# Gated two-branch attention on one core: row halves in strict turn, stacks loaded a string earlier, differences one pair ahead, maxima transposed two bursts later

## The chip, the cores and the metric

The kernel runs on one core of one Trainium2 chip. The metric is the time of one execution in device microseconds (us). The kernel before has a median of 2800.9 us over three runs (2798.58 to 2801.37). Engines are named as in the profile: PE is the matrix engine (PEld its weight loads), DVE the vector engine, ACT the activation engine, POOL the general engine, SP the engine that issues most DMAs.

## The reference

Two attention blocks A and B with weights of their own read the same x, and a gate per token mixes them:

```python
def _A_ref(x, wqkv, wo):
    B, S, D = x.shape                    # 1, 2048, 512
    H = 32
    Dh = D // H                          # 16
    qkv = (lambda x, *d: x.transpose(*d))((x @ wqkv).reshape(B, S, 3, H, Dh), 2, 0, 3, 1, 4)
    q, k, v = qkv[0], qkv[1], qkv[2]
    scores = jnp.einsum("bhqd,bhkd->bhqk", q, k) * (Dh ** -0.5)
    p = _softmax(scores, axis=-1)
    o = jnp.einsum("bhqk,bhkd->bhqd", p, v)
    return (lambda x, *d: x.transpose(*d))(o, 0, 2, 1, 3).reshape(B, S, D) @ wo
...
x = A_x
g = _sigmoid((x * gate_w).sum(-1, keepdims=True))
a = _A_ref(x, A_wqkv, A_wo)
b = _B_ref(x, B_wqkv, B_wo)
return g * a + (1 - g) * b
```

So there are 64 heads (32 of A, 32 of B), each with 2048 x 2048 scores and a head width of 16. The softmax needs the maximum of each row of scores.

## The kernel before, in words

A prologue (to about 328 us) computes q, k and v of both blocks, splits q and k into two half-precision parts each, and writes them to DRAM. From there on the kernel is one long loop over 1024 rounds: 64 heads of 16 rounds. In round r of head h a block of 128 keys meets all 2048 queries.

**Stacks.** For a head, `load_stacks` (lines 103 to 122) puts the parts of q and k into the tiles `q_st` and `k_st`, 48 rows of parts, twice: on partitions 0 to 47 and again on 64 to 111. `x_st` holds differences of key halves. There are three q and k stacks and two of `x_st`, used in turn. The load is twelve DMAs on SP (L115 to L122, six for each half).

**Banks and row halves.** Scores are made one bank (128 x 512) at a time, by four matmuls on the 64-row half 0 or the half 64 of the PE array (`HALVES`), each on 32 columns. `rows()` (line 133) takes the halves in turn: `turn[0]` says which half is next. Matmuls on the two halves can run at the same time. There are four kinds of banks:
- "e", `score` (L218): the transposed scores of a key block; ACT takes the exponential of it (L220) into `p`. The row maxima enter as two more rows of the stack, so the exponent is already shifted.
- "m", `max_plain` (L153, then L159 on DVE): scores of a query block against 512 keys, and their maximum.
- "D", `max_rise` (L153 from `x_st`, then L166 on ACT): the positive part of the difference of two key quarters' scores, written to a buffer `rise`, of which there are three.
- "A", `max_pair` (L153, then L171 on DVE): scores of one quarter plus that `rise`, and the maximum of the sum, which is the maximum over both quarters. L171 writes into the same `rise` buffer.

**Bursts.** `attend` (L698) multiplies p by v in full precision. A head's sums stand in two PSUM tiles, `acc[0]` for half 0 and `acc[1]` for half 64, and a burst of n handles n blocks of 128 queries with both halves alternating, half 0 first. At a head's end ACT copies both tiles out (L721), POOL adds them (L723), and SP stores the sum to `od` (L724).

**The order.** Two rounds, a pair, are one string of steps: `Dmemme3eem2emmeeAe3`, where a digit is a burst. It has 16 banks: D, A, six m and eight e. Ahead of every burst `turn[0]` is set to 0, so the bank behind it takes half 0. An iteration of the loop is two strings, four rounds. The maxima run 24 rounds ahead of the scores that use them: a string whose scores are of round r makes the plain maxima and pairs of round r + 22 and the one behind it, and its "D" makes the difference of round r + 26, two pairs ahead of the "A" that uses it. The prologue makes the first two differences.

**At a head's border.** With r the first round of an iteration:
- r mod 16 = 2: the stacks of head r // 16 + 2 are loaded. On SP this comes behind the store of the head that has just ended. The first "D" of that head comes two strings later.
- r mod 16 = 6: the last maxima of a head are made; `max_split` and `max_rows` are put into `row_ops`, from which one is taken behind each burst.
- `max_split` (line 176): DVE takes the maximum over four columns (L180), POOL scales and splits it (L181 to L183).
- `max_rows` (line 186): DVE transposes the result (L188), SP writes it to DRAM (L191) and reads it back as two rows of `q_st` in both halves (L193). The head's first "e" needs these rows.

**Other work in the loop.** Work with a due round (`later`) is put in by `due`: loads of v for a group of eight heads (POOL's queue), reciprocals of the denominators (four, on DVE, through `row_ops`), and the output projections (L566), four tiles at a time ahead of a burst. The last 22 rounds have no maxima left and their own order.

Of the kernel before, what the change touches and what calls it, by code (L numbers as in the profile page):

```python
# [38 lines left out]
NT = S // P  # L39
# [4 lines left out]
NH = 2 * H  # L44
ROUNDS = NH * NT
# [4 lines left out]
HALVES = (0, 64)  # L50
# [4 lines left out]
def gated_mha(ctx: ExitStack, tc: tile.TileContext, xT, x, wqkv_a, wo_a, wqkv_b, wo_b, gate_w, out):  # L55
# [47 lines left out]
    def load_stacks(h, halves=HALVES):  # L103
        dma = nc.sync.dma_start
        s, hh = divmod(h, H)
        g, j = divmod(hh, HG)
        q, k = q_st[h % 3], k_st[h % 3]
        qs, ks, xs = qd[s][g], kd[s][g], xd[s][g]

        def pairs(t, step, n=S):  # L110
            v = t[0, j]
            return bass.AP(tensor=v.tensor, offset=v.offset, ap=[[n, DH], [step, 2], [1, n]])

        for b in halves:
            dma(k[b:b + 32], pairs(ks, HG * DH * S))  # L115
            dma(q[b:b + 32], pairs(qs, 0))
            dma(k[b + 32:b + 48], ks[0, j])
            dma(q[b + 32:b + 48], qs[1, j])
            if h:
                x = x_st[h % 2]  # L120
                dma(x[b:b + 32], pairs(xs, HG * DH * 512, 512))
                dma(x[b + 32:b + SC], xs[0, j])  # L122
# [6 lines left out]
    FIRST = NT + LEAD + 2  # L129
    mxp, rises = {}, {}  # L130
    turn = [0]

    def rows():
        turn[0] ^= 1
        return HALVES[1 - turn[0]]

    def new_maxima(h):
        mxp[h] = small.tile([P, NT, 4], F32, name="mxp")
        if h:
            pool.memset(mxp[h][:, FIRST % NT if h == 1 else 0::2, 1:2], LOWEST)  # L140

    def scores_bank(m, c, early=False):
        h, t = divmod(m, NT)
        st = c == "rise" or early and c % 2
        ps = (ps_st if st else ps_m).tile([P, 512], F32, name="ps_st" if st else "ps_m")
        b = rows()
        q = q_st[h % 3]
        if c == "rise":
            k = x_st[h % 2][b:b + SC]
        else:  # L150
            k = k_st[h % 3][b:b + SC, c * 512:(c + 1) * 512]
        for j in range(0, P, 32):
            pe.matmul(ps[j:j + 32], q[b:b + SC, t * P + j:t * P + j + 32], k, start=True, stop=True,  # L153
                      tile_position=(b, j))
        return ps, mxp[h][:, t]

    def max_plain(m, c, early=False):
        ps, o = scores_bank(m, c, early)
        dve.tensor_reduce(o[:, c:c + 1], ps, op=ALU.max, axis=AX.X)  # L159
# [3 lines left out]
    def max_rise(m):  # L163
        ps, _ = scores_bank(m, "rise")
        rises[m] = small.tile([P, 512], F32, name="rise", bufs=3)
        act.activation(rises[m], ps, AF.Relu)  # L166

    def max_pair(m):
        ps, o = scores_bank(m, 0)
        rise = rises.pop(m)  # L170
        dve.tensor_tensor_reduce(out=rise, in0=ps, in1=rise, scale=1.0, scalar=LOWEST,  # L171
                                 op0=ALU.add, op1=ALU.max, accum_out=o[:, 0:1])
# [26 lines left out]
    def result_bank():  # L199
        if ring:  # L200
            ring[0] = (ring[0] + 1) % 6
        if not ring or ring[0] % 2:
            return ps_m.tile([P, 512], F32, name="ps_m")
        return ps_st.tile([P, 512], F32, name="ps_st")

    def score(r, c):
        h, kt = divmod(r, NT)
        if c == 0:
            pt[r] = pro.tile([P, S], F32, name="raw") if r < 2 else ppool.tile([P, S], F32, name="p")
        q, k = q_st[h % 3], k_st[h % 3]  # L210
        kk, cc = (4 * (kt % 4) + c, kt // 4) if h == NH - 1 else (kt, c)
        b = rows()
        if r < 2 and c % 2:
            ps = ps_m.tile([P, 512], F32, name="ps_m")
        else:
            ps = result_bank() if ring else ps_st.tile([P, 512], F32, name="ps_st")
        for j in range(0, P, 32):
            pe.matmul(ps[j:j + 32], k[b:b + SC + 2, kk * P + j:kk * P + j + 32],  # L218
                      q[b:b + SC + 2, cc * 512:(cc + 1) * 512], start=True, stop=True, tile_position=(b, j))
        act.activation(pt[r][:, c * 512:(c + 1) * 512], ps, AF.Exp, scale=SCALE / UNIT ** 2)  # L220
# [13 lines left out]
    with tc.tile_pool(name="xs", bufs=1) as xs, tc.tile_pool(name="pro", bufs=2) as pro:  # L234
# [179 lines left out]
        for t in range(NT):  # L414
# [5 lines left out]
            elif t in (11, 13):  # L420
                turn[0] = 0
                for c in range(4):
                    score(t // 2 - 5, c)
        for i in range(2):
            turn[0] = 0
            max_rise(FIRST + 2 * i)
        assert not ahead


# [259 lines left out]
    def attend(r, qa, qb):  # L689
        h, kt = divmod(r, NT)  # L690
        v, j = vg[h // HG], h % HG
        p = pt[r]
        final = h == NH - 1
        a = kt % 4
        first, last = (a == 0, a == 3) if final else (kt == 0, kt == NT - 1)
        for c in range(NQ):
            for i, b in enumerate(HALVES):
                pe.matmul(acc[i][32 * c:32 * c + 17, qa * P:qb * P], v[b:b + 64, 4 * a + c if final else kt, j],  # L698
                          p[b:b + 64, c * 512 + qa * P:c * 512 + qb * P], start=first and qa == 0, stop=last,
                          tile_position=(b, 32 * c), skip_group_check=True)  # L700
        if qb < 4:
            return
        del pt[r]
        if final and last:
            hi = work.tile([P, 512], F32R, name="ev_hi", tag="num")
            lo = work.tile([P, 512], F32R, name="ev_lo")
            ev = work.tile([P, 512], F32, name="ev")
            act.copy(ev, acc[0])
            dve.tensor_tensor(ev, acc[1], ev, op=ALU.add)
            if kt == NT - 1:  # L710
                act.copy(hi, ev)
                dve.tensor_tensor(lo, ev, hi.bitcast(F32), op=ALU.subtract)
            else:
                pool.tensor_copy(hi, ev)
                pool.tensor_tensor(lo, ev, hi.bitcast(F32), op=ALU.subtract)
            tail[kt // 4] = (hi, lo)
        elif last:
            G, j = divmod(h, HG)
            parts = [work.tile([P, 512], F32, name=n) for n in ("ev_lo", "ev")]
            for i in range(2):  # L720
                act.copy(parts[i], acc[i])  # L721
            ev = parts[1]
            pool.tensor_tensor(ev, parts[0], ev, op=ALU.add)  # L723
            nc.sync.dma_start(od[G][j].rearrange("c r t -> (c r) t"), ev)  # L724
# [15 lines left out]
    projects, row_ops = [], []  # L740

    def due(first):
        for r in (first, first + 1):
            for fn, a in later.pop(r, ()):
                if fn is project_out:
                    projects.append(a)
                else:
                    fn(*a)

    first = 2 + NT + LEAD  # L750
    plain = ((m + c // 4, c % 4) for m in range(first, ROUNDS, 2) for c in range(2, 8))
    pairs = iter(range(first, ROUNDS, 2))
    to_rise = iter(range(first + 4, ROUNDS, 2))

    load_stacks(2)
    r = 2
    while r < ROUNDS:
        m = r + NT + LEAD
        if m >= ROUNDS and not ring:
            ring.append(5)  # L760
            turn[0] = 0
        order = (EDGE if r % NT == 2 and r > 2 else FULL)[0] + (EDGE if r % NT == 14 else FULL)[1]
        if m >= ROUNDS:
            order = LATE
        n = order.count("e") // 4
        due(r)
        if r % NT == 2 and r // NT + 2 < NH:
            if r // NT:
                load_stacks(r // NT + 2)
            new_maxima(r // NT + 2)  # L770
        scored = bursts = 0
        for step in order:
            if step == "e":
                if scored == 8:
                    due(r + 2)
                score(r + scored // 4, scored % 4)
                scored += 1
            elif step == "m":
                max_plain(*next(plain))
            elif step == "D":  # L780
                for k in to_rise:
                    max_rise(k)
                    break
            elif step == "A":
                max_pair(next(pairs))
            else:
                for a in projects:
                    project_out(*a)
                projects.clear()
                turn[0] = 0  # L790
                attend_next(int(step))
                if row_ops:
                    fn, *a = row_ops.pop(0)
                    fn(*a)
                for fn, a in mid.pop((r, bursts), ()):
                    fn(*a)
                bursts += 1
        if m < ROUNDS and (m + 4) % NT == 0:
            row_ops += [(max_split, m // NT), (max_rows, m // NT)]
        r += n  # L800
    attend_next(4)
    for fn, a in mid.pop((ROUNDS - 2, 2)):
# [29 lines left out]
```

## Time and profile before

| | us |
|---|---|
| median of three runs | 2800.9 |
| the profiled execution | 2808.05 |
| its span | 2806.3 |
| PE busy | 2657.5 (95%) |
| ACT busy | 2417.1 (86%) |
| DVE busy | 2369.4 (84%) |
| POOL busy | 354.7 (13%) |

Busy time counts an instruction from its start to its end. Consecutive ones overlap on ACT and DVE, and matmuls of different parts of the array run at the same time, so an engine can be busy all the time and still wait. Idle time is put down to the engine whose signal came last. In the timeline equal instructions that follow each other stand in one row with their count.

### The profile page before, as it was taken

To read this page: it belongs to the slowest core of one execution; us is meant where nothing else is said; L and a number is where in the kernel's file an instruction comes from. 1 tells how busy PE (TensorE), PEld (TensorE's weight loads), DVE (VectorE), ACT (ScalarE), POOL (GpSimd) and SP (SyncE) were. 2 spreads that over 40 slices of the span, in tenths; PEclk is the share of its full clock that TensorE was granted. 3 is DMA by queue.
4 is the path that set the end of the run, shared out by engine and by line. 5 is a ranking of instruction groups with operands and counts; after the bars stand their busy time and mean duration, and the time that the engine had idled before them with its cause. 6 is when DMAs were issued, how large, how long until landed. Compare 5 with 4: busy or idle time off the path is not lost.

```text
span 2806.3 us, 147881 instructions
## 1 busy us (share of the span) xinstructions
PE 2657.5 (95%) x66710; PEld 1511.1 (54%) x66710; DVE 2369.4 (84%) x4474; ACT 2417.1 (86%) x4862; POOL 354.7 (13%) x594
## 2 busy tenths in 40 slices
PE   9999999999999999999999999999999999999998
PEld 7777555555455555555455555555555545545553
DVE  4434799999899999999899878899899989998784
ACT  4122799999999999999999878899999999998696
POOL 1010112220000000000100323000000011002212
PEclk9999999999999999999999999999999999999999
DMA  5352212111111111111211212111211121122102
GB/s 197 110 158 96 66 45 65 52 46 38 49 41 31 30 40 49 37 39 37 60 36 32 97 57 75 33 34 29 53 37 38 38 56 42 31 58 75 49 24 93
DMA packets 95934, 159.62 MB, mean 57 GB/s; under 512 B 26182, under 2 KB 43974, under 8 KB 95302
## 3 DMA queue, kind: packets, MB, share of 16 engines
q1 hardware_dynamic: 91590, 139.68, 16.1%
q8 instruction: 522, 8.55, 1.3%
q0 software_dynamic: 2560, 8.91, 1.3%
q10 hardware_dynamic: 1152, 1.57, 0.2%
q14 instruction: 110, 0.90, 0.1%
HBM read 100.56 MB, written 49.54 MB: 53 GB/s over the span
## 4 chain that ended last, share of the span: by engine, by line
PE 42%; ACT 37%; DVE 9%; issue 8%; DMA 2%; POOL 1%; SPq 1%; POOLq 0%; ACTq 0%
ACT p L220 33%; PE acc L698 15%; PE ps_st L218 8%; DVE mxp L159 6%; PE ps_st L298 6%; PE ps_m L153 3%; PE ps_st L351 3%; PE ps_m L566 3%; PE ps_st L153 3%; ACT rise L166 2%; ACT ev_lo L721 2%; DVE rise L171 1%; DMA x_st<-xd 1%; POOL mrow L181 1%; DMA q_st<-qd 1%
## 5 line engine op out<-in xcount | busy, mean ns | idle before, releaser
L220 ACT ACTIVATE p<-ps_st 128x512 f32<-128x512 f32 x4044 | 2055.9, 651 | 98.3 <-PE ps_st L218 86.8
L159 DVE TENSOR_REDUCE mxp<-ps_m 128x1 f32<-128x512 f32 x3048 | 1899.5, 682 | 210.6 <-PE ps_st L153 94.5
L218 PE MATMUL ps_st<-q_st,k_st 50*32 50x512 f16 x16192 | 1517.7, 383 | 86.1 <-ACT p L220 3.9
L698 PE MATMUL acc<-p,vg 64*17 64x384 f32 (+1 forms) x32320 | 1390.4, 382 | 13.3 <-issue 4.4
L153 PE MATMUL ps_m<-k_st,q_st 48*32 48x512 f16 x14192 | 1244.7, 384 | 13.1 <-DVE mxp L171 12.3
L218 PEld LDWEIGHTS <-k_st 50*32 50x32 f16 x16384 | 627.5, 90 | 824.7 <-issue 735.3
L698 PEld LDWEIGHTS acc<-p,vg 64*17 64x17 f32 x32320 | 557.6, 93 | 126.3 <-ACT ev_lo L721 25.0
L153 PEld LDWEIGHTS <-q_st 48*32 48x32 f16 x16384 | 436.3, 90 | 239.6 <-issue 162.7
L166 ACT ACTIVATE rise<-ps_st 128x512 f32<-128x512 f32 x500 | 306.4, 613 | 50.8 <-DVE mxp L171 30.7
L171 DVE CUSTOM_DVE_ANT_0 rise<-ps_m,rise 128x512 f32<-128x512 f32 x500 | 340.3, 681 | 1.3 <-PE ps_m L153 1.3
L153 PE MATMUL ps_st<-x_st,q_st 48*32 48x512 f16 x2000 | 201.4, 378 | 14.8 <-DMA q_st<-qd 7.7
L723 POOL TENSOR_TENSOR ev<-ev_lo,ev 128x512 f32<-128x512 f32 x63 | 80.2, 1274 | 1057.0 <-ACT ev L721 1057.0
L181 POOL TENSOR_SCALAR mrow<-mrow 128x16 f32<-128x16 f32 x64 | 16.4, 256 | 992.7 <-DVE mrow L180 992.7
L318 ACT ACTIVATE parts<-ps_st 128x512 f16<-128x512 f32 x64 | 38.0, 596 | 112.1 <-PE ps_st L298 105.4
L319 DVE SCALAR_TENSOR_TENSOR parts<-ps_st,parts 128x512 f16<-128x512 f32 x64 | 44.0, 690 | 96.1 <-ACT parts L318 89.9
L354 ACT COPY v_st<-ps_st 128x512 f32<-128x512 f32 x32 | 18.8, 586 | 99.0 <-PE ps_st L351 96.6
L566 PE MATMUL ps_m<-wo,ot 128*128 128x512 f32 x348 | 85.5, 401 | 2.7 <-DVE mxp L159 2.7
L566 PEld LDWEIGHTS ps_m<-wo,ot 128*128 128x128 f32 x348 | 65.8, 192 | 23.4 <-issue 8.7
L298 PE MATMUL ps_st<-xh,whi 128*128 128x512 f32 x224 | 59.9, 390 | 0.0
L298 PE MATMUL ps_st<-xh,wlo 128*128 128x512 f32 x224 | 59.9, 390 | 0.0
L298 PE MATMUL ps_st<-xl,whi 128*128 128x512 f32 x224 | 59.9, 390 | 0.0
L553 POOL TENSOR_TENSOR o_num<-o_num,rb 128x512 f32<-128x512 f32 x28 | 35.7, 1280 | 95.6 <-DMA rb<-rd 95.6
(120 smaller groups left out, 1005.2 us busy)
## 6 DMA issues: line engine op xcount, KB each, us to landing
k_st<-kd SPq DMA_DIRECT2D x128, 128.0 KB
q_st<-qd SPq DMA_DIRECT2D x128, 128.0 KB
od<-ev SPq DMA_DIRECT2D x63, 256.0 KB
vd<-v_st SPq DMA_DIRECT2D x32, 272.0 KB
vg<-vd POOLq DMA_DIRECT2D x32, 272.0 KB, 4.6
qd<-parts SPq DMA_DIRECT2D x32, 256.0 KB
kd<-parts SPq DMA_DIRECT2D x32, 256.0 KB
k_st<-kd SPq DMA_DIRECT2D x128, 64.0 KB
```

Source lines behind the costliest of these rows:

```text
L153: pe.matmul(ps[j:j + 32], q[b:b + SC, t * P + j:t * P + j + 32], k, start=True, stop=True, tile_position=(b, j))
L159: dve.tensor_reduce(o[:, c:c + 1], ps, op=ALU.max, axis=AX.X)
L166: act.activation(rises[m], ps, AF.Relu)
L171: dve.tensor_tensor_reduce(out=rise, in0=ps, in1=rise, scale=1.0, scalar=LOWEST, op0=ALU.add, op1=ALU.max, accum_out=o[:, 0:1])
L218: pe.matmul(ps[j:j + 32], k[b:b + SC + 2, kk * P + j:kk * P + j + 32], q[b:b + SC + 2, cc * 512:(cc + 1) * 512], start=True, stop=True, ti ...
L220: act.activation(pt[r][:, c * 512:(c + 1) * 512], ps, AF.Exp, scale=SCALE / UNIT ** 2)
L298: pe.matmul(ps, w[a][:, k], (xh, xl)[b][cc][:, k], start=n == 0, stop=n == 3 * KC - 1)
L351: pe.matmul(ps, a[:, k, o:o + P], b[:, k], start=n == 0, stop=n == 3 * KC - 1)
L566: pe.matmul(ps, ot[a][:, slot, tt * P:(tt + 1) * P], wt[b][:, g], start=first and i == 0, stop=last and i == 2)
L698: pe.matmul(acc[i][32 * c:32 * c + 17, qa * P:qb * P], v[b:b + 64, 4 * a + c if final else kt, j], p[b:b + 64, c * 512 + qa * P:c * 512 + ...
L721: act.copy(parts[i], acc[i])
L723: pool.tensor_tensor(ev, parts[0], ev, op=ALU.add)
```

## The change

Four edits. The line numbers behind them fall by one or two.

```diff
-        for i in range(2):
-            turn[0] = 0
-            max_rise(FIRST + 2 * i)
+        max_rise(FIRST)
...
         for c in range(NQ):
-            for i, b in enumerate(HALVES):
+            for i in (turn[0], 1 - turn[0]):
+                b = HALVES[i]
                 pe.matmul(acc[i][32 * c:32 * c + 17, qa * P:qb * P], v[b:b + 64, 4 * a + c if final else kt, j],
...
-    to_rise = iter(range(first + 4, ROUNDS, 2))
+    to_rise = iter(range(first + 2, ROUNDS, 2))
...
         if r % NT == 2 and r // NT + 2 < NH:
-            if r // NT:
-                load_stacks(r // NT + 2)
             new_maxima(r // NT + 2)
...
                 if scored == 8:
                     due(r + 2)
+                    if (r + 2) % NT == 0 and r // NT + 3 < NH:
+                        load_stacks(r // NT + 3)
...
-                turn[0] = 0
                 attend_next(int(step))
                 if row_ops:
                     fn, *a = row_ops.pop(0)
-                    fn(*a)
+                    if fn:
+                        fn(*a)
...
-            row_ops += [(max_split, m // NT), (max_rows, m // NT)]
+            row_ops += [(max_split, m // NT), (None,), (None,), (max_rows, m // NT)]
```

**Halves.** `turn[0]` is no longer set to 0 ahead of a burst, and a burst begins with the half whose turn it is. In the string, six banks stand ahead of the first burst, three ahead of the second and seven ahead of the third. Before, the bank just ahead of the second and of the third burst was on half 0, and the burst began with half 0 too; the bank behind the burst took half 0 again. Now two neighbours never share a half. Since the prologue makes one difference and not two, each "D" falls on half 64. On PE, at the third burst of a string, before (acc_74 belongs to half 0, acc_75 to half 64):

```order
L218 LDWEIGHTS k_st_163
L218 MATMUL ps_st<-q_st_162,k_st_163 32x512
L698 MATMUL acc_74<-p,vg 17x384
L698 MATMUL acc_75<-p,vg 17x384
L698 MATMUL acc_74<-p,vg 17x384
```

And now:

```order
L218 LDWEIGHTS k_st_163
L218 MATMUL ps_st<-q_st_162,k_st_163 32x512
L697 MATMUL acc_75<-p,vg 17x384
L697 MATMUL acc_74<-p,vg 17x384
L697 MATMUL acc_75<-p,vg 17x384
```

The score ahead of the burst is on half 0 in both; the burst began with half 0 and now begins with half 64, and so does the "D" behind it.

**Differences.** "D" makes the difference of the next pair and not of the one behind that. With three buffers, the one it writes was last read by an "A" two strings back; before, by the "A" of the string just ended.

**Maxima.** Between `max_split` and `max_rows` two bursts are passed without a row operation. On DVE at the border of a head, before (L159 is a plain maximum, the two rows of L171 are one pair):

```order
L180 TENSOR_REDUCE mrow<-mxp 128x16
L159 TENSOR_REDUCE mxp<-ps_m 128x1
L188 STREAM_TRANSPOSE mt<-mparts 128x32
L159 TENSOR_REDUCE mxp<-ps_m 128x1 x2
L171 ISA rise,mxp<-ps_m,rise 128x512
L171 ISA mxp 128x1
L159 TENSOR_REDUCE mxp<-ps_m 128x1 x6
```

And now:

```order
L180 TENSOR_REDUCE mrow<-mxp 128x16
L159 TENSOR_REDUCE mxp<-ps_m 128x1 x3
L171 ISA rise,mxp<-ps_m,rise 128x512
L171 ISA mxp 128x1
L159 TENSOR_REDUCE mxp<-ps_m 128x1 x3
L188 STREAM_TRANSPOSE mt<-mparts 128x32
L159 TENSOR_REDUCE mxp<-ps_m 128x1 x3
```

The transpose moved behind five more maxima and the pair between them.

**Stacks.** The load of head h + 3's stacks is issued in the middle of the iteration r mod 16 = 14, just behind the last scores of head h, whose stack it overwrites. On SP around a head's border, before:

```order
L191 DMA md_114<-mt 4x32x32
L193 DMA q_st_2668<-md_114 2x2048 x2
L724 DMA od_108<-ev 128x512
L115 DMA k_st_168<-kd_90 32x1x2048
L116 DMA q_st_167<-qd_82 32x1x2048
```

And now:

```order
L191 DMA md_114<-mt 4x32x32
L193 DMA q_st_2661<-md_114 2x2048 x2
L115 DMA k_st_168<-kd_90 32x1x2048
L116 DMA q_st_167<-qd_82 32x1x2048
L117 DMA k_st_168<-kd_90 16x2048
```

The store of the ended head's sums (L724, now L723) stood ahead of the twelve loads and now stands behind them.

## The prediction

> **What bounds the kernel now.** I read the page first, then ACT's time by stage, then what ACT waited for in each stage, then single pairs of rounds in the timeline, and last the queue of SP. By the page's shares PE, DVE and ACT are all nearly full, which does not tell which one sets the pace. The timeline of ACT over one pair in the middle of a head tells it (start, length, line, count):
>
> ```profile
> 1513.72 1.17 ACT L220 ACTIVATE p<-ps_st 128x512 f32<-128x512 f32 x2
> 1514.81 0.60 ACT L166 ACTIVATE rise<-ps_st 128x512 f32<-128x512 f32 x1
> 1515.30 4.02 ACT L220 ACTIVATE p<-ps_st 128x512 f32<-128x512 f32 x8
> 1519.22 0.60 ACT L166 ACTIVATE rise<-ps_st 128x512 f32<-128x512 f32 x1
> ```
> ```profile
> 1515.30 0.59 ACT L220 ACTIVATE p<-ps_st 128x512 f32<-128x512 f32 x1
> ```
>
> Eight exponentials end 4.02 - 0.59 = 3.43 us apart from first to last, so ACT finishes one in 0.490 us when it is fed. A pair has nine operations: 9 x 0.490 = 4.41, and the two rises end at 1515.41 and 1519.82, 4.41 apart. So in the middle of a head ACT is already full. A head is 64 exponentials, 8 rises and 2 copies of the accumulators: 74 x 0.490 = 36.26 us. What a head takes is seen from one transpose (L188) to the next:
>
> ```profile
> 1113.76 0.21 DVE L188 STREAM_TRANSPOSE mt<-mparts 128x32 f16<-128x32 f16 x1 [0.35 <-POOL mparts L183]
> ```
> ```profile
> 1148.74 3.54 ACT L220 ACTIVATE p<-ps_st 128x512 f32<-128x512 f32 x7
> 1149.60 0.21 DVE L180 TENSOR_REDUCE mrow<-mxp 128x16 f32<-128x64 f32 x1
> 1149.72 0.68 DVE L159 TENSOR_REDUCE mxp<-ps_m 128x1 f32<-128x512 f32 x1
> 1150.76 0.21 DVE L188 STREAM_TRANSPOSE mt<-mparts 128x32 f16<-128x32 f16 x1 [0.35 <-POOL mparts L183]
> 1150.89 1.25 DVE L159 TENSOR_REDUCE mxp<-ps_m 128x1 f32<-128x512 f32 x2
> 1150.99 0.57 SPq L191 DMA_DIRECT2D md<-mt  x1
> 1152.05 0.68 DVE L171 CUSTOM_DVE_ANT_0 rise<-ps_m,rise 128x512 f32<-128x512 f32 x1
> 1152.84 0.60 ACT L166 ACTIVATE rise<-ps_st 128x512 f32<-128x512 f32 x1 [0.55 <-DVE mxp L171]
> 1152.97 0.52 SPq L193 DMA_DIRECT2D q_st<-md  x2
> ```
>
> It is 37.00, so 0.74 over ACT's floor, and the rows show nearly all of it in one place: the last exponential ends at 1152.28, the rise ends at 1153.44 and not 0.49 later, a loss of 0.67. The rise waited for L171 (end 1152.73), which frees the rise buffer it is to write; L171 was late because DVE had stood still for POOL (0.35) before L188.
>
> How much ACT loses in all is its count at 0.490 against each stage's length (us, then busy and count), with what it waited for in the first and third stage:
>
> ```profile
> 327.70:1604.00 1276.30, 1241.45 (x2516) 0.99 0.16 46
> 1604.00:1799.00 195.00, 147.17 (x299) 1.00 0.19 58
> 1799.00:2512.00 713.00, 693.80 (x1407) 1.00 0.15 42
> 2512.00:2694.30 182.30, 147.04 (x298) 0.98 0.19 57
> ```
> ```profile
> ACT rise L166 <- DVE mxp L171: 18.2, 35, 0.6
> ACT rise L166 <- PE ps_m L153: 8.3, 4, 3.4
> ACT p L220 <- PE ps_st L218: 4.2, 6, 1.0
> ACT rise L166 <- PE ps_st L153: 2.5, 1, 2.5
> ```
> ```profile
> ACT rise L166 <- PE ps_m L153: 6.3, 3, 2.5
> ACT p L220 <- PE ps_st L218: 1.9, 2, 1.0
> ```
> ```profile
> ACT p L220 <- PE ps_st L218: 45.1, 4, 11.3
> ```
> ```profile
> ACT p L220 <- PE ps_st L218: 29.3, 5, 8.8
> ACT p L220 <- PE ps_m L153: 5.5, 3, 2.8
> ```
>
> The first stage loses 1276.3 - 1232.8 = 43.5, the third 713.0 - 689.4 = 23.6. The second loses 48.5, of which 45.1 stand behind the four output projections (last but one fence), leaving 3.4; the fourth loses 36.3, of which 34.8 (last fence) are of that sort, leaving 1.5. Together 72.0 us are in reach of the change. Of them 8.3 + 4.2 + 2.5 + 6.3 + 1.9 = 23.2 belong to rises that waited for a matmul, and to exponentials just behind them; these are the heads whose stacks came late.
>
> **The strict turn.** PE's last burst of a string (L698) and the start of the next string, and DVE beside it:
>
> ```profile
> 1513.49 1.02 PE L698 MATMUL acc<-p,vg 64*17 64x384 f32 x16
> 1514.15 0.43 PE L153 MATMUL ps_m<-k_st,q_st 48*32 48x512 f16 x4
> 1514.33 0.40 PE L153 MATMUL ps_st<-x_st,q_st 48*32 48x512 f16 x4
> ```
> ```profile
> 1514.77 0.40 PE L153 MATMUL ps_m<-k_st,q_st 48*32 48x512 f16 x4
> 1514.94 0.40 PE L218 MATMUL ps_st<-q_st,k_st 50*32 50x512 f16 x4
> ```
> ```profile
> 1514.63 0.08 DVE L171 DVE_READ_ACCUMULATOR2_ANT mxp<- 128x1 f32 x1
> 1514.84 3.68 DVE L159 TENSOR_REDUCE mxp<-ps_m 128x1 f32<-128x512 f32 x6
> ```
>
> The last "e" and the first matmuls of the burst behind it (1513.49) now share a half, and "D" needs the same half: its matmuls start at 1514.33, after those of the "m" behind it in the program, which took the other half at 1514.15. They end at 1514.73, and the rise could not start before about 1514.78, which is also where ACT's turn falls (1514.89 + 0.49 - 0.60). So "D" is on the edge. With strict turn "D" takes the half that is free first, starts at about 1514.15 and is 0.18 early; "m" then starts at 1514.33, and since DVE's first reduction waited for "D" until 1514.84, it starts when it did. PE executes as many matmuls as before. The second and third burst change places of halves in the same way, where PE has to wait for ACT's banks anyway. Behind a head's end the first burst now begins with the accumulator that is copied second; the exponentials of the two copies' time cover that. By itself this edit is worth 0.00 to 0.03 a pair, at most 500 x 0.03 = 15 us; I count it in the sum only as what keeps the next edit from stopping at "D".
>
> **Differences one pair ahead.** Three rise buffers stay. The rise now overwrites the one that L171 read two strings ago, not one, so that wait has a whole pair (4.41) of room. No work is added; one rise moves from the prologue into the loop: +0.5.
>
> **Maxima transposed two bursts on.** DVE's insertion was 1150.89 - 1149.60 less one reduction of 0.60, so 0.69, in one place. Now L180 costs 0.12 (1149.60 to 1149.72) and L188 0.13 (1150.76 to 1150.89), a pair apart, and POOL's work lies beside reductions. DVE has 0.13 idle a pair (1514.71 to 1514.84 above). Its delay reaches ACT only by the third "m" (1514.77, waits for L171's bank) and the "e" behind it (1514.94): 0.17 of room. I take 0.05 a head, 62 x 0.05 = 3; bounds 0 and 62 x 0.25 = 16. In the seven heads with reciprocals these now follow L188 burst upon burst: 2, bounds 0 and 7 x 0.6 = 4 (one reduction's time a head).
>
> What is late next is the scores of the next head, which need the maxima's rows:
>
> ```profile
> 1161.42 0.40 PE L218 MATMUL ps_st<-q_st,k_st 50*32 50x512 f16 x4
> ```
>
> L188 to this matmul: 10.66. L188 moves by three reductions, L171 and three more, 0.12 + 1.80 + 0.81 + 1.80 - 1.16 = 3.4, and ACT's 0.67 goes: 6.6 stay. Needed: L188 to the second L193 is 2.5 (1150.76 to about 1153.23), and a write of the same 8 KB took 1.98 from issue until L193 could start (1150.99 to 1152.97): 4.5. Room 2.1. Behind these DMAs on SP wait only the next stack's, which are due later.
>
> **Stacks at a head's first round.** The load's first DMA stands behind the store of od on SP; its time, and the old head's last score on PE:
>
> ```profile
> 1507.87 0.56 SPq L115 DMA_DIRECT2D k_st<-kd  x1
> ```
> ```profile
> 1499.24 0.40 PE L218 MATMUL ps_st<-q_st,k_st 50*32 50x512 f16 x4
> ```
>
> Now it waits only for the old head's last score, the matmuls of 1499.24: 8.2 earlier. The first use, "D" of the new head, comes one string later: 4.4. Together 12.6 us of room where the longest wait was 3.4. Twelve issues, 6.7 us at L115's 0.56, now stand ahead of od's store; they are through about when it was ready (8.2 later), and its reader is behind it on SP anyway.
>
> **The sum.** 72.0 less 0.5, 3, 2 and 3 for strays that I cannot place: 63.5. The profiled execution took 2808.05 (span 2806.3), so 2744.5 there. The median is 2800.9, 7.15 below; if that whole difference is load waits that profiling lengthened, the gain is 56, if none of it, 63.5. I take 2738.
>
> The Trainium skill speaks against all this: by "ScalarE: Activation LUTs", What ACT_TABLE_LOAD costs, an ACTIVATE with immediate scale and bias takes 186 ns + 0.833 ns an element and overlaps its neighbour by 93, so 520 ns here, and a head could not be under 38.5; by it ACT has nothing to lose and the time stays. The trace disagrees (0.490, and heads of 37.00).
>
> **The rivals.**
> - *The delay comes back through PE.* DVE's two inserts, though apart, push the third "m" and so the exponentials, and half of 62 x 0.67 returns: +21, 2759. For it: the room is only 0.17, and PE is in order. 0.15.
> - *Loads stay late.* The group's value loads share the DMA engines with the stacks, and they now begin together: +23, 2761. Against: 12.6 of room. 0.07.
> - *More goes.* Of the fourth stage 34.8 - 3 x 8.8 = 8.4 are not projections: 2730. 0.08.
> - *Slower: the maxima land late.* At the first "e" of each head PE waits for L193. It pays from 6.6 us after L188, and eats the whole gain from 7.6 (62 x 1.0). Once the trace shows that much:
>
> ```profile
> 1701.98 0.55 SPq L191 DMA_DIRECT2D md<-mt  x1
> 1708.15 0.53 SPq L193 DMA_DIRECT2D q_st<-md  x2
> ```
>
>   There the path is 0.24 + 6.17 + 0.26 + 1.98 = 8.65. In every head this would be 62 x 2.05 = 127: 2865. Against: output loads filled the queue there. 0.05.
> - *No change.* ACT's 74 operations fill a head by themselves, at 37.00 / 74 = 0.50 each, and the 0.67 only moves to another wait of ACT: 2800. Against: pairs of 4.41. 0.05. The page above is of this side.
>
> **The numbers.** The forecast has 0.60, at 2738 with bounds 2729 (all 72 kept) and 2753 (the inserts at 16, the reciprocals at 4). With the rivals up to 2761 the range is 2726 to 2764. About 0.2% (5.6 us) can be told from no change: faster 0.90, same 0.05, slower 0.05.
>
> **What would show it.** L188 without idle time before it; rises that wait for L171 gone; the "D" matmuls ahead of the next "m"; heads of 36.3 to 36.5 from one L188 to the next; no rise that waits over 1 us for a matmul. It is wrong if the exponentials wait for L218 once in each head, or if ACT's operations in a pair end more than 4.41 apart.

## The result, and the profile after

The changed kernel takes 2724.1 us (median of four runs, 2723.3 to 2724.6); the kernel before took 2801.1 on the same chip (2798.6 to 2804.3). The ratio is 0.9724, with a 95% interval of 0.9707 to 0.9741, so it is faster by 77 us. The forecast was 2738 and its range began at 2726: the direction and the main mechanism hold, but the gain is larger than the range allowed. The profiled execution of the changed kernel took 2724.6 (span 2722.8), that of before 2808.0: 83.5 between the two profiles, where the sum gave 63.5.

The page's groups of the two lines that stood at the rise buffer. The last figures are the idle time ahead of them:

```profile
L166 ACT ACTIVATE rise<-ps_st 128x512 f32<-128x512 f32 x500 | 357.2, 715 | 0.0
L171 DVE CUSTOM_DVE_ANT_0 rise<-ps_m,rise 128x512 f32<-128x512 f32 x500 | 340.6, 681 | 0.0
```

Over 500 rises ACT never waited for one. The timeline at a head's border shows why, DVE first, then ACT, then PE's line L153:

```profile
1123.70 0.21 DVE L180 TENSOR_REDUCE mrow<-mxp 128x16 f32<-128x64 f32 x1
1123.83 1.88 DVE L159 TENSOR_REDUCE mxp<-ps_m 128x1 f32<-128x512 f32 x3
1125.62 0.68 DVE L171 CUSTOM_DVE_ANT_0 rise<-ps_m,rise 128x512 f32<-128x512 f32 x1
1126.23 0.08 DVE L171 DVE_READ_ACCUMULATOR2_ANT mxp<- 128x1 f32 x1
1126.31 1.89 DVE L159 TENSOR_REDUCE mxp<-ps_m 128x1 f32<-128x512 f32 x3
1128.11 0.20 DVE L188 STREAM_TRANSPOSE mt<-mparts 128x32 f16<-128x32 f16 x1
```
```profile
1126.19 0.72 ACT L166 ACTIVATE rise<-ps_st 128x512 f32<-128x512 f32 x1
1126.68 4.14 ACT L220 ACTIVATE p<-ps_st 128x512 f32<-128x512 f32 x8
1130.60 0.72 ACT L166 ACTIVATE rise<-ps_st 128x512 f32<-128x512 f32 x1
```
```profile
1125.67 0.42 PE L153 MATMUL ps_st<-x_st,q_st 48*32 48x512 f16 x4
1125.86 0.40 PE L153 MATMUL ps_m<-k_st,q_st 48*32 48x512 f16 x4
```

L188 no longer stands still for POOL (no bracket behind it). The rise of 1126.19 starts while L171 of this pair is still at work, since it fills another buffer. "D" (the first PE row) runs ahead of the next "m". The next rise comes 4.41 later: a pair at a head's border is now as short as one in the middle. The next head's transpose:

```profile
1164.38 0.20 DVE L188 STREAM_TRANSPOSE mt<-mparts 128x32 f16<-128x32 f16 x1
```

1164.38 - 1128.11 = 36.27: the floor of 74 x 0.490 = 36.26. ACT's time by stage (start and end, length, busy and count, PE's granted clock, share and GB/s of DMA), and then all that ACT waited for from 329.4 to 2623 (total, times, longest):

```profile
329.40:1527.50 1198.10, 1197.56 (x2444) 1.00 0.16 46
1527.50:1718.00 190.50, 145.12 (x296) 1.00 0.22 67
1718.00:2444.70 726.70, 726.08 (x1481) 1.00 0.15 43
2444.70:2621.20 176.50, 145.21 (x296) 1.00 0.19 57
```
```profile
ACT p L220 <- PE ps_st L218: 77.3, 8, 11.5
```

At 0.490 each, the operations of the first stage need 1197.6 of 1198.1, those of the third 725.7 of 726.7. Over the whole loop ACT waits eight times, for the eight groups of output projections (four of four tiles, three of three and one of two: 27 tiles, 2.86 each). Beside these it loses about 0.24 in each of the seven heads with reciprocals. PE itself waits 0.57 once a head, 35.5 in all, for the second copy of the accumulators (`ev`, L720), since the first burst now begins there. The prediction said that ACT's exponentials would cover this, and they do: ACT has no wait for it.

### The profile page after: what moved, and what is told of

It is laid out like the page before. It is cut to its first block, busy times and chain, and to the rows that moved or that the text cites. A ratio compares the mean times of both kernels' runs of the same rounds, so it can differ in the third digit from the quotient of the medians.

```text
span 2722.8 us, 147771 instructions
## 1 busy us (share of the span) xinstructions
PE 2577.0 (95%) x66710; PEld 1521.8 (56%) x66710; DVE 2361.3 (87%) x4474; ACT 2401.3 (88%) x4862; POOL 355.4 (13%) x594
## 4 chain that ended last, share of the span: by engine, by line
PE 73%; ACT 17%; DVE 7%; issue 2%; DMA 1%; SPq 0%; DVEq 0%; ACTq 0%
PE acc L697 30%; PE ps_st L218 20%; ACT p L220 15%; PE ps_m L153 9%; PE ps_st L298 6%; DVE mxp L159 6%; PE ps_st L351 3%; PE ps_m L564 3%; ACT ev L720 2%; PE ps_st L153 1%; DVE rise L171 1%; DMA x_st<-xd 0%; DVE rn L520 0%; DMA raw<-in_xT 0%; PE ps_st L564 0%
## 5 line engine op out<-in xcount | busy, mean ns | idle before, releaser
L220 ACT ACTIVATE p<-ps_st 128x512 f32<-128x512 f32 x4044 | 2105.1, 725 | 82.3 <-PE ps_st L218 77.8
L159 DVE TENSOR_REDUCE mxp<-ps_m 128x1 f32<-128x512 f32 x3048 | 1893.0, 682 | 160.5 <-PE ps_m L153 64.8
L697 PE MATMUL acc<-p,vg 64*17 64x384 f32 (+1 forms) x32320 | 1367.6, 379 | 39.3 <-ACT ev L720 35.5
L153 PE MATMUL ps_m<-k_st,q_st 48*32 48x512 f16 x14192 | 1118.7, 380 | 1.7 <-DVE mxp L171 1.3
L218 PEld LDWEIGHTS <-k_st 50*32 50x32 f16 x16384 | 636.8, 89 | 834.4 <-issue 712.9
L153 PEld LDWEIGHTS <-q_st 48*32 48x32 f16 x16384 | 444.1, 89 | 145.8 <-issue 57.0
L166 ACT ACTIVATE rise<-ps_st 128x512 f32<-128x512 f32 x500 | 357.2, 715 | 0.0
L171 DVE CUSTOM_DVE_ANT_0 rise<-ps_m,rise 128x512 f32<-128x512 f32 x500 | 340.6, 681 | 0.0
L153 PE MATMUL ps_st<-x_st,q_st 48*32 48x512 f16 x2000 | 210.4, 377 | 0.0
L298 PEld LDWEIGHTS ps_st<-xh,wlo 128*128 128x128 f32 x224 | 42.0, 188 | 8.8
```

What stands on the lines that cost most here:

```text
L298: pe.matmul(ps, w[a][:, k], (xh, xl)[b][cc][:, k], start=n == 0, stop=n == 3 * KC - 1)
```

## The experiments

Times are medians of four runs; the kernel before, run beside them in four groups, had 2801, 2803, 2802 and 2802. Each diff is against the kernel named.

### One edit undone

**no_turn**: the changed kernel with the fixed halves.

```diff
-            for i in (turn[0], 1 - turn[0]):
-                b = HALVES[i]
+            for i, b in enumerate(HALVES):
...
+                turn[0] = 0
                 attend_next(int(step))
```

> The changed kernel with the halves as before (turn set to 0 ahead of each burst, a burst begins with half 0). Theory of the prediction: the D matmuls fall back to about 0.18 us later, on the edge of ACT's turn, but no longer behind a wait for L171, so 0.00 to 0.03 us a pair: 2724 to 2739 us, likeliest 2726, heads of 36.26 to 36.5 us. Rival, that the steady pairs owe their time to the strict turn: heads lose 0.3 us or more, 2745 us or more.

Measured 2726.9, ratio 0.9735 (0.9720 to 0.9749). The intervals of the two ratios overlap, so the 2.8 more are not clear of the noise: beside the other three edits the turn is worth almost nothing.

**no_later_maxima**: the transpose one burst behind the maxima.

```diff
-            row_ops += [(max_split, m // NT), (None,), (None,), (max_rows, m // NT)]
+            row_ops += [(max_split, m // NT), (max_rows, m // NT)]
```

> The changed kernel with the transpose one burst behind the maxima, as before. Theory of the prediction: DVE again loses 0.69 us at one place; with the rise free of L171 some 0.35 us of it is covered, so 0.34 us a head comes back: 62 x 0.34 = 21, about 2745 us. Rival A, the free rise buffer alone hides all of it: 2724 us. Rival B, the whole 0.67 us returns: 2765 us.

Measured 2751.2, ratio 0.9819 (0.9804 to 0.9833): 27 more. Heads take 36.68. The rise buffer is free in time, yet the stop of DVE before L188 still reaches ACT, now through PE and the exponentials. ACT's waits from 329 to 1527:

```profile
ACT p L220 <- PE ps_st L218: 6.7, 32, 0.2
```

Each head loses 36.68 - 36.26 = 0.42, and this row shows 6.7 / 32 = 0.21 of it. So differences one pair ahead do not by themselves cure the stop before L188; the later transpose is needed for that.

**no_near_rise**: differences two pairs ahead.

```diff
-        max_rise(FIRST)
+        for i in range(2):
+            max_rise(FIRST + 2 * i)
...
-    to_rise = iter(range(first + 2, ROUNDS, 2))
+    to_rise = iter(range(first + 4, ROUNDS, 2))
```

> The changed kernel with differences two pairs ahead again. Theory of the prediction: each rise waits for the L171 of the string just ended, on the edge of ACT's turn; 0.02 us a pair (about 8 us) and DVE's two inserts of 0.12 and 0.13 us go to ACT in full (62 x 0.25 = 16): about 2748 us, rises that wait for L171 in the trace. Rival, the buffer does not matter once the transpose is moved: 2724 to 2728 us.

Measured 2734.2, ratio 0.9761 (0.9746 to 0.9775): 10 more, where the theory had 24. Once the transpose has moved, little is left for the buffer to make late; the price I gave DVE's two inserts was too high. The edit is not a pure one: with two differences in the prologue every "D" also falls on half 0 again (PE's wait for `ev` is gone), and what that half is worth here no run tells apart.

**no_early_load**: the stacks loaded at the old place.

```diff
+            if r // NT:
+                load_stacks(r // NT + 2)
             new_maxima(r // NT + 2)
...
-                    if (r + 2) % NT == 0 and r // NT + 3 < NH:
-                        load_stacks(r // NT + 3)
```

> The changed kernel with the stacks loaded at the old place, behind the store of od. Theory of the prediction: the first D of a head still comes one string later, 4.4 us of room against a longest wait of 3.4, so waits for stacks stay away: 2724 to 2727 us. What is open: between 2512 and 2694 us of the kernel before ACT lost some 8 us that I had left out of the sum; if they came from the stacks loaded together with the output loads, they return here: about 2732 us. Rival, the early load is what cures the late stacks: 18 us or more return, 2742 us.

Measured 2745.8, ratio 0.9803 (0.9787 to 0.9820): 21.6 more. My theory, that a use 4.4 us later is room enough, fell, and the rival held. Four rows of what PE waited for, from 329 to 2700:

```profile
PE ps_m L153 <- issue: 5.0, 4, 1.6
PE ps_st L153 <- DMA x_st<-xd: 2.5, 5, 0.7
PE ps_st L218 <- issue: 2.5, 2, 1.6
PE acc L697 <- issue: 2.2, 3, 1.4
```

Only 2.5 are waits for the stack. The rest is marked "issue": PE stood still and no signal of the profile was due. The same view of the changed kernel from 329 to 2650 has no such row.

### One edit alone

Each is the kernel before with the lines of that edit from the diff of the change.

**only_near_rise**

> The kernel before with the differences one pair ahead and nothing else. Theory: the insert of 0.69 costs ACT 0.42 a head as in the changed kernel without the later transpose, not 0.67: 62 x 0.25 = 16; the small losses of 0.02 at the rises go (5), and the first D of a head has 4.4 us more for its stacks (15 of the waits): 2801 - 36 = 2765 us. Rival, D on the edge of its row half holds the rises: 2785 us.

Measured 2763.4, ratio 0.9867 (0.9842 to 0.9892). 39.7 saved, a little more than the 36 expected: heads of 36.74. PE no longer waits for a stack, but 6.1 us of its stops marked "issue" stay.

**only_later_maxima**

> The kernel before with the transpose two bursts later and nothing else. Theory: DVE's insert falls from 0.69 to 0.12 and 0.13 us, and with the rise still bound to L171 both reach ACT: 0.25 to 0.30 a head instead of 0.67, so 62 x 0.4 = 25 less: 2776 us. Rival, the rise buffer is what counts and nothing is won alone: 2799 us.

Measured 2776.1, ratio 0.9912 (0.9887 to 0.9937): 26.9 saved, as expected. The shortest heads take 36.46 (before: 36.99), but the waits for stacks stay.

**only_early_load**

> The kernel before with the stacks loaded at the head's first round and nothing else. Theory now: the late stacks cost more than the 23 us of waits that the prediction counted, since PE also stops for 1 to 2 us without any wait that the trace names while stacks and output loads are in flight; taking the early load out of the changed kernel cost 21.6 us. So 2801 - 28 = 2773 us, and the stops of PE between 2500 and 2690 us gone. By the prediction's own price 23 us: 2778 us, stops still there. Rival, the place of the load is worth only what the trace calls a DMA wait beyond 4.4 us: 2795 us.

Measured 2772.7, ratio 0.9896 (0.9866 to 0.9926): 30.4 saved, and the rises go on waiting for L171 as before (heads of 36.99). PE no longer waits for a stack, and its stops marked "issue" fall from 7.6 to 1.5 us. The late stacks were worth more than the 23.2 of the prediction.

**only_turn**

> The kernel before with the strict turn alone. Theory: the two neighbours that shared a half cost nothing by themselves, since the exponentials keep ACT full in the middle of a head and the late rise of a head still waits for the rise buffer; so 2796 to 2804, the same as the kernel before within its spread, heads still 36.9 to 37.0. Rival: each pair gains up to 0.03 us, 500 x 0.03 = 15: 2786.

Measured 3051.9, ratio 1.0905 (1.0880 to 1.0931): 250 us slower, 4.0 a head, against a forecast of no change. PE's waits from 329 to 1527, and SP around one head's load:

```profile
PE ps_st L153 <- DMA x_st<-xd: 89.5, 29, 5.1
```
```profile
1220.06 0.54 SPq L121 DMA_DIRECT2D x_st<-xd  x1
1220.65 0.58 SPq L122 DMA_DIRECT2D x_st<-xd  x1
...
1224.47 0.54 SPq L121 DMA_DIRECT2D x_st<-xd  x1
1225.06 0.58 SPq L122 DMA_DIRECT2D x_st<-xd  x1
```
```profile
1220.12 0.71 ACT L166 ACTIVATE rise<-ps_st 128x512 f32<-128x512 f32 x1
1220.61 4.14 ACT L220 ACTIVATE p<-ps_st 128x512 f32<-128x512 f32 x8
1228.16 0.60 ACT L166 ACTIVATE rise<-ps_st 128x512 f32<-128x512 f32 x1 [3.41 <-PE ps_m L153]
```

A head's first "D" waits for x_st. The strict turn put every "D" on half 64, and half 64's x_st is loaded by the second six DMAs, 4.4 later than half 0's. The rise due at 1224.5 comes at 1228.16.

### Half or turn

**turn_first_half**: the strict turn alone, with the parity shifted by leaving out the reset in the prologue, so that "D" is on half 0 again.

```diff
         for i in range(2):
-            turn[0] = 0
             max_rise(FIRST + 2 * i)
```

> The kernel before with the strict turn alone, but with the parity of the turns shifted by one, so that each difference D is on half 0 as before. Theory (the 250 us of the strict turn alone are the wait of D on half 64 for the second six loads): 2796 to 2804, no change, heads of 36.9 to 37.0. Rival (the strict turn itself collides with something): about 3050.

Measured 2795.1 (ten runs), ratio 0.9975 (0.9961 to 0.9989): 7 us faster, 0.014 a pair on average. The 7 do not sit in each pair, though: pairs in the middle of a head take 4.41 as before, and a head takes 36.88 instead of 36.99, 62 x 0.11 = 6.8.

**loads_swapped**: the kernel before, with nothing but the order of the two sets of six loads changed.

```diff
-        for b in halves:
+        for b in halves[::-1]:
```

> The kernel before with one change: a head's six loads for half 64 are issued ahead of the six for half 0. No turn is changed, D stays on half 0. Theory (D waits for whichever half is loaded second, about 4.4 us later): as with the strict turn alone, 62 heads by about 4.0: 3000 to 3060. Rival (the strict turn itself was the cause): 2796 to 2806.

Measured 3076.9, ratio 1.0975 (1.0952 to 1.0998). With turn_first_half: the order of the loads against the half of "D" is the cause, and the turn itself does no harm.

**turn_early_load**: the kernel before with the strict turn and the early load.

> The kernel before with the strict turn and the early load. D is on half 64, needing loads that land 4.4 us later, but they begin 8.2 us earlier. Theory: 3.8 us to spare, so the same as the early load alone (2773): 2762 to 2780. Rival (the strict turn costs by itself): 2800 and more.

Measured 2763.3, ratio 0.9860 (0.9845 to 0.9874): the early load makes the half harmless.

**late_first_half**: no_early_load with "D" on half 0.

```diff
         max_rise(FIRST)
+        turn[0] ^= 1
```

> The changed kernel with the loads at the old place, and the parity of the turns shifted so that D is on half 0, whose loads land first. Theory A (PE's stops come while the stack loads are in flight, wherever D stands): most of the 21.6 us that the old place of the loads cost stay, 2738 to 2746. Theory B (the cost was D's wait for the half that lands last, and the half clock behind it): 2724 to 2730.

Measured 2738.7, ratio 0.9770 (0.9755 to 0.9785). Of the 21.6 that the old place cost, 7 went with the half and 14.5 stayed, and with them PE's stops, from 329 to 2650:

```profile
PE acc L698 <- issue: 4.6, 3, 2.6
PE ps_m L153 <- issue: 2.6, 4, 1.3
```

Theory A holds for the larger part.

### How late the maxima may come

**four_bursts_on** and **six_bursts_on**: the changed kernel with four or six bursts passed between the two row operations, where the change passes two. The edit for six:

```diff
-            row_ops += [(max_split, m // NT), (None,), (None,), (max_rows, m // NT)]
+            row_ops += [(max_split, m // NT), *[(None,)] * 6, (max_rows, m // NT)]
```

> The changed kernel with the transpose another two bursts later (four empty places between max_split and max_rows). Theory of the prediction: 2.1 us are left between the landing of the maxima's rows and the next head's first score; L188 moves by three reductions and L171, 2.5 to 3.0 us, so the scores wait 0.4 to 0.9 us in each head: 62 x 0.65 = 40, about 2764 us, with a wait of L218 for the rows in each head. Rival, there is more room than worked out: 2724 us; or much less: over 2790 us.

Measured 2724.0, ratio 0.9725 (0.9702 to 0.9749): no loss, and the expectation was wrong.

> The changed kernel with six bursts passed between the two row operations. With four the transpose stood 6.81 us behind L180 and the first score of the head began 4.3 us behind the transpose, while the rows had landed at 3.7; two bursts more put the transpose at 1.16 + 2 x 4.41 = 9.98 behind L180, 3.17 later, so the first score would be due 1.1 behind it. Theory (the slower rival of the prediction is real, only farther off): PE then waits 2.6 us for the rows in each head, ACT's stock covers 0.7 to 1.4 of it, and 62 heads lose 1.2 to 1.9: 2798 to 2842, likeliest 2820. Rival (PE gets ahead of ACT far enough to take the wait): 2724 to 2745.

Measured 2931.2, ratio 1.0468 (1.0445 to 1.0491): worse than expected. The transpose and the head's first exponentials, in the changed kernel, with four and with six:

```profile
1128.11 0.20 DVE L188 STREAM_TRANSPOSE mt<-mparts 128x32 f16<-128x32 f16 x1
...
1135.51 1.21 ACT L220 ACTIVATE p<-ps_st 128x512 f32<-128x512 f32 x2
```
```profile
1130.03 0.21 DVE L188 STREAM_TRANSPOSE mt<-mparts 128x32 f16<-128x32 f16 x1
...
1135.02 1.69 ACT L220 ACTIVATE p<-ps_st 128x512 f32<-128x512 f32 x3
```
```profile
1208.38 1.09 ACT L220 ACTIVATE p<-ps_st 128x512 f32<-128x512 f32 x2 [2.01 <-PE ps_m L153]
```

With the change the exponentials start 7.40 behind the transpose, with four bursts 4.99 behind it and still in time. With six they can start no sooner than 4.62 behind it (the transpose was at 1203.76), and PE has waited. So the change has about 2.8 of room (7.40 - 4.62), and the two more bursts of four_bursts_on use 2.4 of it. But the wait costs more than itself. PE's waits with six, from 329 to 1527, and all engines in and behind one such wait (length, then busy and count of PE, PEld, DVE, ACT, POOL, then PE's granted clock):

```profile
PE ps_st L218 <- DMA q_st<-md: 67.3, 31, 2.4
```
```profile
1206.00:1208.40 2.40, 0.53 (x24) 0.34 (x32) 0.48 (x2) 0.39 (x2) 0.00 (x0) 1.00 0.20 53
1208.40:1212.00 3.60, 3.60 (x100) 2.29 (x92) 2.63 (x5) 2.99 (x6) 0.00 (x0) 0.58 0.46 129
1212.00:1216.00 4.00, 3.38 (x108) 1.90 (x94) 3.22 (x8) 4.00 (x9) 1.34 (x2) 0.95 0.30 82
```

PE waits 67.3 / 31 = 2.2 a head, the clock is then 0.58 in the mean of the next 3.6, and the head loses (2931.2 - 2724.0) / 62 = 3.3 in all. The slower rival of the prediction exists; it starts two to four bursts further on.

### Smaller pieces of projection

**one_tile_a_burst** puts one tile ahead of a burst in place of all that are due; **one_tile_a_string** makes them due two rounds sooner and puts one ahead of each third burst. The edit of the first:

```diff
-                for a in projects:
-                    project_out(*a)
-                projects.clear()
+                if projects:
+                    project_out(*projects.pop(0))
```

> The changed kernel with one output projection tile ahead of a burst instead of all that are due. Each tile of 12 matmuls takes PE about 2.85 us; all 27 stand on the path now, about 77 us over ACT's floor in the two stages. Theory (ACT has a stock of about 1.2 us of finished banks when PE turns to a tile, and PE rebuilds part of it between two bursts): each tile loses 0.8 less, 27 x 0.8 = 22: 2702. Rival (PE has no time to spare, so the packing does not matter): 2724.

> The changed kernel with the tiles made due two rounds earlier and one ahead of each string's third burst. Theory (the stock is whole again after a string): each of the tiles behind the first of a group loses 1.2 less, about 20 x 1.2 to 27 x 1.6 = 24 to 43: 2681 to 2700, likeliest 2692. Rival (PE has no time to spare): 2724.

Measured 2733.2 (ratio 0.9759, 0.9742 to 0.9777) and 2729.3 (0.9744, 0.9723 to 0.9764). Both theories fell: neither gains, both lose a little. One tile of the second kernel, on PE and on ACT:

```profile
1559.46 3.01 PE L564 MATMUL ps_m<-wo,ot 128*128 128x512 f32 x12
1562.40 0.86 PE L697 MATMUL acc<-p,vg 64*17 64x384 f32 x16
```
```profile
1557.39 3.17 ACT L220 ACTIVATE p<-ps_st 128x512 f32<-128x512 f32 x6
1563.52 0.60 ACT L166 ACTIVATE rise<-ps_st 128x512 f32<-128x512 f32 x1 [2.96 <-PE ps_m L153]
```

The tile keeps PE for 2.94 and ACT loses 2.96. ACT's stock does reach to 1560.56, 1.1 past the tile's start, but the burst behind the tile (the second PE row) needs that stock in every string anyway. So PE has no spare time that smaller pieces could use, and no kernel here beats the changed one.

## Why the prediction was right in kind and too small

Where the gain lies can be read from the end of every 64th exponential in the two traces. Some of these 65 points, with the profile's time before and after and the gain so far:

```
exponentials   before    after    gain
          64    339.7    337.5    2.21
        1792   1348.2   1317.8   30.43
        1856   1390.5   1354.0   36.50
        1920   1427.7   1390.3   37.37
        3584   2448.3   2380.0   68.28
        3904   2669.2   2588.3   80.86
        3968   2711.6   2630.0   81.56
        4095   2788.0   2704.8   83.14
```

An ordinary head gains 0.73, a head with late stacks up to 6.07 (the third row). From 64 to 3968 that makes 79.35: 61 x 0.73 = 44.5 and 34.8 above it, where the sum had 23.2 for late stacks. By the four stages of the prediction, with the gain read at their borders in the same way ("forecast" is what the sum held to be in reach there):

| from to, before | forecast | measured |
|---|---|---|
| first stage, 327.7 to 1604 | 43.5 | 42.57 |
| second stage, to 1799 | 3.4 | 3.16 |
| third stage, to 2512 | 23.6 | 23.76 |
| fourth stage, to 2694.3 | 1.5 | 10.05 |
| deductions | -8.5 | in the rows above |
| ahead of the first stage and behind the fourth | 0 | 3.94 |
| sum | 63.5 | 83.5 |

So the 20.0 that the sum was short of are 8.6 in the fourth stage, 7.5 of deductions that did not come, and 3.9 outside the four stages, for which the sum had no term.

**The bound by ACT, and the ordinary head.** Right. The heads came down to 36.26, and the waits named as signs went.

**The deductions.** Too large: 0.5 + 3 + 2 + 3 = 8.5, but the first three stages gained 69.5 of the 70.5 in reach, so only about 1.0 of it came. DVE's two inserts cost nothing (heads of 36.27 with both in them); the reciprocals' 2 came as 7 x 0.24 = 1.7; nothing of the 3 for strays is seen.

**The fourth stage.** This is the step that failed most. "34.8 (last fence) are of that sort", that is, output projections, was taken from the engine and line that released ACT. The window held three groups of three tiles (the group of two lies behind its end). The same three after the change, from 2444.7 to 2621.2:

```profile
ACT p L220 <- PE ps_st L218: 26.2, 3, 8.7
```

The other 34.8 - 26.2 = 8.6 were PE's stops and their followers. PE's waits in the fourth stage of the kernel before show four stops marked "issue", 6.7 in all, and in that of the changed kernel there is none:

```profile
PE acc L698 <- issue: 3.8, 2, 2.0
PE ps_st L218 <- issue: 2.9, 2, 1.6
```

One of them in the timeline of the kernel before, and the windows around it:

```profile
2595.44 0.41 PE L698 MATMUL acc<-p,vg 64*17 64x128 f32 x10
2597.89 0.83 PE L698 MATMUL acc<-p,vg 64*17 64x128 f32 x19 [2.04 <-issue]
```
```profile
2595.00:2597.90 2.90, 0.86 (x33) 0.30 (x21) 1.94 (x5) 1.64 (x4) 1.54 (x4) 1.00 0.53 160
2597.90:2600.00 2.10, 2.10 (x46) 1.17 (x46) 0.55 (x1) 0.55 (x2) 0.36 (x1) 0.50 0.24 66
```

That these stops belong to the loads at the old place is shown by only_early_load and no_early_load. The rival "more goes" had this term, 8.4, at a chance of 0.08. The range took it (2730) and the case of no deductions (2729) one at a time; both came, and 72.0 + 8.4 would have put its lower end at about 2720. The profile had the sign for it: eight waits in the two rows where there are three groups of tiles.

**Late stacks.** In the first three stages the sum held, but the share of the late stacks in it was larger than 23.2: about 27.7 (34.8 less what the four heads of the fourth stage gained above the ordinary 0.73, 10.05 - 4 x 0.73 = 7.1). A wait there was dearer than its row. The head of the table's third row, before:

```profile
1364.13 0.62 PE L153 MATMUL ps_st<-x_st,q_st 48*32 48x512 f16 x4 [3.07 <-DMA q_st<-qd]
```
```profile
1362.30:1369.10 6.80, 4.97 (x104) 2.84 (x108) 2.58 (x4) 2.66 (x5) 0.00 (x0) 0.50 0.21 55
```
```profile
1364.79 0.60 ACT L166 ACTIVATE rise<-ps_st 128x512 f32<-128x512 f32 x1 [3.35 <-PE ps_m L153]
...
1367.35 1.08 ACT L220 ACTIVATE p<-ps_st 128x512 f32<-128x512 f32 x2 [0.99 <-PE ps_st L218]
1369.12 2.06 ACT L220 ACTIVATE p<-ps_st 128x512 f32<-128x512 f32 x4 [0.68 <-PE ps_st L218]
```

A wait of 3.35 at the rise is followed by 0.99 and 0.68 at half clock; I had the first and part of the others. That "4.4 later" and "8.2 earlier" add to room was right, but they are not alike: the early load alone removes PE's waits for stacks and its stops over 0.8 (only_early_load), while the later use alone leaves stops of up to 1.6 (only_near_rise, no_early_load).

**The strict turn.** "0.00 to 0.03 a pair" holds for the turn itself as an average (0.014), though not where it was expected: the gain lies at the head's border. The step overlooked the half on which "D" comes to stand, and so the load it needs; alone, the edit costs 250. The early load hid this: that the forecast was not hurt by it is luck.

**The room for the maxima.** 2.1 was the estimate and about 2.8 the measured room; the wait beyond it cost 1.5 times its length (3.3 against 2.2 a head), with the half clock behind it.

**Median and profile.** The gain in medians is 6.5 below that in profiles, within the 0 to 7.15 that the prediction allowed for. Its 2738 took almost none of it, and so in medians the forecast is 14 short and not 20.

The parts do not add: alone they save 39.7, 30.4, 26.9 and 7 (the turn with "D" kept on half 0), together 104, where the change saves 77. At L188 differences one pair ahead and the later transpose nearly add: heads of 36.99 become 36.74 and 36.46, 0.25 and 0.53 less, and with both 36.26, 0.73 less. The greater overlap is in the late stacks: of the 39.7 only 62 x 0.25 = 16 lie in the ordinary heads, so some 24 go the way of the 30.4 of the early load, and what could be had there is about 35. The rest of the overlap is not worked out.

## What to carry to other kernels

A wait is put down to the signal that came last, so a count of waits that doesn't fit the number of pieces of work (eight waits, three groups) is a reason to look at each one before the stage is written off as fixed cost. An edit that only renames a resource, here the half of a matmul, changes which transfer it depends on: look up when each copy lands. Price a stop of PE with the clock behind it, not by its length alone.

## What the runs showed of the hardware

- **Half clock after short stops.** PE's granted clock fell to 0.50 behind stops of 2.04, 2.47 and 3.07 us, for 6.8 us in the longest case quoted (of which 1.8 the end of the stop itself). The Trainium skill, "TensorE: Matmul & The Clock Gate", Why this matters for your kernels, advises no gaps over about 3 us. Here shorter ones were enough, and their length alone does not decide: in the kernel before, stops of 1.51 and 1.55 us (ended at 2010.51 and 1553.25) were followed by 0.50 for 3.41 us, stops of 1.61 and 1.65 (ended at 2551.75 and 2462.94) by 1.00.
- **Stops without a signal.** PE stood still for 0.9 to 2.6 us with nothing due, 24 times from 329 to 2700 in six kernels that load the stacks at the old place; only_turn and loads_swapped load there too and have none over 0.8, and stops of up to 0.8 came in some others. The packets of the traces have 16-KB loads on the instruction queue, 4.6 us apart in the median of the kernel before. Each of the 24 stops ends 1.3 to 1.7 behind the landing of such a load, and that load had started 6.6 to 8.4 behind the one ahead of it. For the stop of 2595.85 to 2597.89 the loads started at 2587.41 and 2595.34, and the second landed at 2596.49. So PE had very likely run out of instructions behind the data loads, but no run changes the instruction loads alone.
- **PE and ACT are full together.** ACT ends an operation every 0.490 us, yet 2.94 of extra work on PE cost ACT 2.96.
